# Two small first chunks, w_in in halves of columns, V by heads, and a new task list in an attention-then-MLP kernel

## The chip, the cores and the metric

The kernel runs on one core of a Trainium2 chip. The metric is device time in microseconds (us) for one launch. TensorE is called PE, VectorE DVE, ScalarE ACT, GpSimd POOL and SyncE SP, as in the profile.

## The reference

```python
def phi(x):                                   # 32 -> 64 features a token
    a = np.einsum('rd,bhsd->bhsr', S1, x)     # r = 8
    b = np.einsum('rd,bhsd->bhsr', S2, x)
    return np.einsum('bhsi,bhsj->bhsij', a, b).reshape(*x.shape[:-1], r * r)
q_p, k_p = phi(q), phi(k)                     # q, k, v: 4 x 4 x 1088 x 32, float32
kv  = np.einsum('bhsf,bhsd->bhfd', k_p, v)
z   = np.sum(k_p, axis=2)
num = np.einsum('bhsf,bhfd->bhsd', q_p, kv)
den = np.einsum('bhsf,bhf->bhs', q_p, z)[..., None] + 1e-06
x   = (num / den), heads side by side: 4352 tokens x 128
h   = x @ w_in                                # 128 x 2048
out = (h * sigmoid(h)) @ w_out                # 2048 x 128
```

Batch 0 has to be worked up into `x` before the MLP can start; the MLP of the first tokens then runs beside the attention of the later batches.

## The kernel before

Every step is a named task, and `ORDER` is a list of all tasks written out by hand. Each engine takes its instructions in the order in which its tasks stand there; the engines wait for each other by semaphores only where data or a buffer is needed. A name carries the batch (0 to 3) or chunk, and the piece.

Loads, all issued by SP: `LK`, `LQ`, `LV` (k, q, v of a batch), `LI` (w_in), `LO` (w_out). Each load's issue waits until the load eight places earlier has landed. `LV` loads V in four loads of 32 partitions each, all heads in one (`load_v`, line 207).

Attention of batch b, in pieces of 64-token groups (`PIECES`; batch 0 has three pieces, the first of 384 tokens):

- `KT` transposes k (DVE), `PK` projects it (PE, into the PSUM tile `pair`), `TK` transposes it back (DVE), `KP` forms the features (DVE for batch 0, POOL in nine parts for the others), `VB` casts V (ACT for batches 0 and 1), `KV` sums k features times v (PE), `KM`, `SE`, `KC` mask, select and copy that sum into the tile `KV`. `ZS`, `ZT`, `MW`, `WM` make the weights for the denominator.
- For each piece of q: `QT` transposes (DVE), `PQ` projects (PE, into `pair`), `TQ` transposes back (DVE, reads `pair`), `AW`, `RD`, `RC`, `AQ` form and apply the reciprocal of the denominator, `QP` forms the features, `TN` transposes them (all DVE), `NM` multiplies with `KV` (PE, into `pair`), and `XC` copies the result as bf16 into `xT` (ACT for batches 0 and 1, DVE for 2 and 3).

So `pair` is taken in turn by `PK`, `PQ` and `NM`, and freed by `TK`, `TQ` and `XC`.

MLP: the tokens are cut into chunks (`SIZES`). For a chunk, `H` multiplies with columns of w_in into one of two PSUM tiles `hp`, `A` applies silu on ACT (two, four or eight columns blocks at once, up to 1,024 elements a partition), `O` multiplies with w_out and accumulates, `F` writes out. From chunk 7 on (`H3`) `pair` is a third tile for `H`. `wi` casts w_in in four quarters on ACT, `wo` casts w_out on POOL. `H0.0` needs the first columns of w_in and `XC0.0`.

`f.0` to `f.106` are matmuls on zeros on PE, whose results nobody reads. They stand in the list up to the first chunk. All matmuls have one line in the profile, 181, as they go through one helper; products on DVE and POOL have line 192.

Of the kernel before, what the change touches and what calls it, by code (L numbers as in the profile page):

```python
# [40 lines left out]
SIZES = [384, 512, 512, 512, 512, 512, 512, 512, 256, 128]  # L41
NG = 8
PIECES = [[(0, 6), (6, 12), (12, 17)], [(0, 8), (8, 17)], [(0, 8), (8, 17)], [(0, 8), (8, 17)]]
KN = [[('D', 0, 5), ('D', 5, 9)], [('P', 0, 1), ('P', 1, 2), ('P', 2, 3), ('P', 3, 4), ('P', 4, 5), ('P', 5, 6), ('P', 6, 7), ('P', 7, 8), ('P', 8, 9)], [('P', 0, 1), ('P', 1, 2), ('P', 2, 3), ('P', 3, 4), ('P', 4, 5), ('P', 5, 6), ('P', 6, 7), ('P', 7, 8), ('P', 8, 9)], [('P', 0, 1), ('P', 1, 2), ('P', 2, 3), ('P', 3, 4), ('P', 4, 5), ('P', 5, 6), ('P', 6, 7), ('P', 7, 8), ('P', 8, 9)]]
XENG = ['AAA', 'AA', 'DD', 'DD']
KVENG = 'AADD'
VB_ENG = 'AAPP'
FILL = {'f.0': (1, 128), 'f.1': (1, 128), 'f.2': (1, 128), 'f.3': (1, 128), 'f.4': (1, 128), 'f.5': (1, 128), 'f.6': (1, 128), 'f.7': (1, 128), 'f.8': (1, 128), 'f.9': (1, 128), 'f.10': (1, 128), 'f.11': (1, 128), 'f.12': (1, 128), 'f.13': (1, 128), 'f.14': (1, 128), 'f.15': (1, 128), 'f.16': (1, 128), 'f.17': (1, 128), 'f.18': (1, 128), 'f.19': (1, 128), 'f.20': (1, 128), 'f.21': (1, 128), 'f.22': (1, 128), 'f.23': (1, 128), 'f.24': (1, 128), 'f.25': (1, 128), 'f.26': (1, 128), 'f.27': (1, 128), 'f.28': (1, 128), 'f.29': (1, 128), 'f.30': (1, 128), 'f.31': (1, 128), 'f.32': (1, 128), 'f.33': (1, 128), 'f.34': (1, 128), 'f.35': (1, 128), 'f.36': (1, 128), 'f.37': (1, 128), 'f.38': (1, 128), 'f.39': (1, 128), 'f.40': (1, 128), 'f.41': (1, 128), 'f.42': (1, 128), 'f.43': (1, 128), 'f.44': (1, 128), 'f.45': (1, 128), 'f.46': (1, 128), 'f.47': (1, 128), 'f.48': (1, 128), 'f.49': (1, 128), 'f.50': (1, 128), 'f.51': (1, 128), 'f.52': (1, 128), 'f.53': (1, 128), 'f.54': (1, 128), 'f.55': (1, 128), 'f.56': (1, 128), 'f.57': (1, 128), 'f.58': (1, 128), 'f.59': (1, 128), 'f.60': (1, 128), 'f.61': (1, 128), 'f.62': (1, 128), 'f.63': (1, 128), 'f.64': (1, 128), 'f.65': (1, 128), 'f.66': (1, 128), 'f.67': (1, 128), 'f.68': (1, 128), 'f.69': (1, 128), 'f.70': (1, 128), 'f.71': (1, 128), 'f.72': (1, 128), 'f.73': (1, 128), 'f.74': (1, 128), 'f.75': (1, 128), 'f.76': (1, 128), 'f.77': (1, 128), 'f.78': (1, 128), 'f.79': (1, 128), 'f.80': (1, 128), 'f.81': (1, 128), 'f.82': (1, 128), 'f.83': (1, 128), 'f.84': (1, 128), 'f.85': (1, 128), 'f.86': (1, 128), 'f.87': (1, 128), 'f.88': (1, 128), 'f.89': (1, 128), 'f.90': (1, 128), 'f.91': (1, 128), 'f.92': (1, 128), 'f.93': (1, 128), 'f.94': (1, 128), 'f.95': (1, 128), 'f.96': (1, 128), 'f.97': (1, 128), 'f.98': (1, 128), 'f.99': (1, 128), 'f.100': (1, 128), 'f.101': (1, 128), 'f.102': (1, 128), 'f.103': (1, 128), 'f.104': (1, 128), 'f.105': (1, 128), 'f.106': (1, 128)}
# [4 lines left out]
WIN = 1  # L53
ENDS = 2
LAST = [8, 6, 2]
DIRECT = [8, 9]
OPS = [5, 7, 9]
H3 = 7
ORDER = """
S2 LK0.0 LK0.1 begin KT0.0 KT0.1 LQ0.0 QT0.0 LV0.0 LV0.1 LV0.2 LV0.3 begin2 S1 f.0 f.1 f.2 f.3 f.4 f.5 f.6  # L60
f.7 f.8 f.9 SM SN table WQ0 WK L4 f.10 f.11 f.12 f.13 f.14 f.15 f.16 f.17 f.18 f.19 f.20 f.21 f.22 f.23 f.24
PK0.0 PK0.1 TK0.0 TK0.1 f.25 f.26 f.27 f.28 f.29 f.30 f.31 f.32 f.33 ZS0 ZT0 f.34 f.35 f.36 f.37 f.38 f.39
f.40 f.41 MW0 WM0 f.42 f.43 f.44 f.45 f.46 f.47 f.48 f.49 f.50 PQ0.0 KP0.0 KP0.5 TQ0.0 AW0.0 RD0.0 RC0.0
AQ0.0 QP0.0 TN0.0 VB0 f.51 f.52 f.53 f.54 f.55 f.56 f.57 f.58 KV0.0 KV0.5 KM0 f.59 f.60 f.61 f.62 f.63 f.64
f.65 f.66 f.67 SE0 KC0 f.68 f.69 f.70 f.71 f.72 f.73 f.74 f.75 f.76 f.77 f.78 f.79 f.80 f.81 f.82 f.83 f.84
f.85 f.86 f.87 f.88 f.89 f.90 NM0.0 LI.0 wi.0 wi.2 wi.3 XC0.0 wi.1 LQ0.1 LO.0 LO.1 wo.1 wo.0 wo.2 wo.3 WR
LK1 LV1.0 LV1.1 LV1.2 LV1.3 QT0.1 QT0.2 f.91 f.92 f.93 f.94 f.95 f.96 f.97 f.98 f.99 f.100 PQ0.2 TQ0.2 AW0.2
RD0.2 RC0.2 f.101 H0.0 H0.1 A0.0 f.102 PQ0.1 f.103 f.104 f.105 f.106 H0.2 O0.0 A0.1 TQ0.1 AW0.1 AQ0.2 RD0.1
QP0.2 RC0.1 TN0.2 AQ0.1 KT1 QP0.1 LQ1 LK2 LV2.0 LV2.1 LV2.2 LV2.3 LQ2 LK3 H0.3 A0.2 O0.1 H0.4 A0.3 A0.4 O0.2
H0.5 A0.5 NM0.2 O0.3 H0.6 XC0.2 H0.7 A0.6 A0.7 PK1 O0.4 O0.5 O0.6 TK1.1 TK1.0 TN0.1 KP1.0 KP1.1 KP1.2 KP1.3  # L70
KP1.4 KP1.5 KP1.6 KP1.7 KP1.8 ZS1 VB1 ZT1 NM0.1 O0.7 MW1 KV1.0 WM1 QT1.0 LV3.0 LV3.1 LV3.2 LV3.3 LQ3 XC0.1
H1.0 A1.0 H1.1 KV1.1 KV1.2 PQ1.0 KV1.3 KV1.4 H1.2 F0 QT1.1 O1.0 A1.1 KV1.5 H1.3 A1.2 A1.3 TQ1.0 AW1.0 RD1.0
KT2 RC1.0 KV1.6 O1.1 H1.4 O1.2 KV1.7 KV1.8 H1.5 PK2 A1.4 KM1 A1.5 H1.6 SE1 O1.3 O1.4 O1.5 H1.7 AQ1.0 QP1.0
TK2.0 TK2.1 TN1.0 A1.6 KC1 NM1.0 XC1.0 A1.7 O1.6 ZS2 PQ1.1 H2.0 ZT2 A2.0 O1.7 H2.1 KT3 TQ1.1 AW1.1 F1 MW2
PK3 WM2 RD1.1 RC1.1 TK3.1 AQ1.1 QP1.1 TK3.0 TN1.1 QT2.0 QT3.0 A2.1 H2.2 A2.2 KP2.0 KP2.1 KP2.2 KP2.3 KP2.4
KP2.5 VB2 KP2.6 KP2.7 VB3 KP2.8 KP3.0 KP3.1 KP3.2 KP3.3 KP3.4 KP3.5 KP3.6 KP3.7 KP3.8 H2.3 O2.0 A2.3 KV2.0
KV2.1 KV2.2 KV2.3 KV2.4 KV2.5 O2.1 H2.4 O2.2 A2.4 H2.5 O2.3 KV2.6 KV2.7 NM1.1 H2.6 A2.5 H2.7 KV2.8 O2.4
XC1.1 A2.6 ZS3 PQ2.0 ZT3 A2.7 KM2 H3.0 O2.5 O2.6 O2.7 SE2 H3.1 TQ2.0 AW2.0 QT2.1 RD2.0 RC2.0 F2 A3.0 A3.1
H3.2 KC2 PQ2.1 MW3 A3.2 KV3.0 H3.3 A3.3 KV3.1 O3.0 H3.4 KV3.2 O3.1 H3.5 O3.2 A3.4 A3.5 TQ2.1 AQ2.0 QP2.0
TN2.0 H3.6 A3.6 NM2.0 XC2.0 AW2.1 RD2.1 RC2.1 AQ2.1 QP2.1 TN2.1 KV3.3 H3.7 A3.7 O3.3 KV3.4 H4.0 O3.4 KV3.5  # L80
H4.1 O3.5 A4.0 KV3.6 H4.2 A4.1 O3.6 H4.3 O3.7 KV3.7 A4.2 H4.4 A4.3 NM2.1 KV3.8 H4.5 F3 WM3 XC2.1 O4.0 A4.4
A4.5 H4.6 PQ3.0 H4.7 O4.1 A4.6 H5.0 QT3.1 TQ3.0 PQ3.1 AW3.0 TQ3.1 KM3 RD3.0 AW3.1 RC3.0 A4.7 H5.1 A5.0 O4.2
H5.2 O4.3 SE3 KC3 AQ3.0 QP3.0 TN3.0 RD3.1 A5.1 H5.3 A5.2 O4.4 H5.4 O4.5 O4.6 A5.3 H5.5 A5.4 O4.7 H5.6 NM3.0
O5.0 A5.5 H5.7 XC3.0 RC3.1 A5.6 A5.7 O5.1 H6.0 O5.2 O5.3 H6.1 A6.0 O5.4 H6.2 A6.1 A6.2 AQ3.1 QP3.1 TN3.1 F4
NM3.1 O6.0 XC3.1 H6.3 O5.5 A6.3 H6.4 A6.4 O5.6 H7.0 A7.0 H6.5 O6.1 H6.6 O6.2 O6.3 O5.7 A6.5 H6.7 H7.3 A6.6
F5 A6.7 H7.1 A7.1 A7.3 O6.4 O6.5 H7.2 O6.6 O7.0 H7.4 O6.7 H7.6 A7.2 H7.5 O7.1 A7.4 A7.6 H7.7 O7.2 O7.3 O7.4
A7.5 F6 A7.7 H8.0 A8.0 H8.1 O7.5 H8.2 O7.6 A8.1 A8.2 H8.3 A8.3 O7.7 H9.0 O8.0 O8.1 H9.1 O8.2 O8.3 H9.2 A9.0
F7 A9.1 A9.2 O9.0 O9.1 O9.2 F8 F9
# [4 lines left out]
def kernel(  # L93
# [77 lines left out]

    def load(name, make):
        def issue():
            landed[name] = make()
            if name in HOLDS:
                tc.add_manual_dep(landed[name].ins, landed[HOLDS[name]].ins.name, mybir.DependencyInfo(
                    mybir.DependencyClass.Sync, mybir.DependencyReason.DATA), reason="order of loads")
        o.add(name, issue)

    def mm(dst, w, x, start=True, stop=True, pos=None, **kw):  # L180
        nc.tensor.matmul(dst, w, x, start=start, stop=stop, tile_position=pos, **kw)  # L181
# [25 lines left out]
    def load_v(b, c):  # L207
        n = min(NC, NY - c * NC)
        return nc.sync.dma_start(
            view(Vx[b % 2][32 * c: 32 * (c + 1), :], 0, (NC * D, H), (1, n * D)),  # L210
            AP(tensor=v.tensor, offset=v[b, 0, c * NC].offset,
               ap=[[NY * D, 32], [S * D, H], [1, n * D]]))

    quarter = DFF // 4
    YQ = 2 * PIECES[0][0][1]
    load("LK0.0", lambda: load_rows(k, Kx, 0, 0, 2 * NC, by[K_ENG]))
    load("LK0.1", lambda: load_rows(k, Kx, 0, 2 * NC, NY))
    load("LQ0.0", lambda: load_rows(q, Qx, 0, 0, YQ))
    load("LQ0.1", lambda: load_rows(q, Qx, 0, YQ, NY))
    for b in range(B):  # L220
        for c in range(4):
            load(f"LV{b}.{c}", lambda b=b, c=c: load_v(b, c))
# [3 lines left out]
    for i in range(WIN):  # L226
        r0, r1 = i * P // WIN, (i + 1) * P // WIN
        load(f"LI.{i}", lambda r0=r0, r1=r1: nc.sync.dma_start(w_in_f[r0:r1, :], moe_w_in[r0:r1, :]))
# [32 lines left out]
    def begin2():  # L261
        nc.gpsimd.tensor_copy(out=view(SEL[:, :], 0, (P, 2), (64, 2), (1, 64)),
                              in_=view(ident[:, :], 0, (1, 2), (0, 2), (2, 64)))
        nc.gpsimd.memset(view(Vx[1][96:P, :], (NY - 3 * NC) * D, (NC * D, H),
                              (1, (4 * NC - NY) * D)), 0.0)
        nc.gpsimd.memset(view(AW[1][:, :], 8, (9, 2 * NN)), 1e-6)
        for b in range(1, B):
            nc.gpsimd.memset(view(WQ[b][:, :], 16, (32, 2), (1, 16)), 0.0)
            nc.gpsimd.memset(view(Kx[b][:, :], NY * D, (1, (4 * NC - NY) * D)), 0.0)
    o.add("begin2", begin2)  # L270
# [75 lines left out]
    def batch(b, kn, pieces, xeng, kveng):  # L346
# [72 lines left out]
        for p, (n0, n1) in enumerate(pieces):  # L419
# [3 lines left out]

            o.add(f"QT{b}.{p}", lambda n0=n0, n1=n1: nc.vector.transpose(  # L424
                out=qt[:, n0 * 64: n1 * 64], in_=Qx[b][:, n0 * 64: n1 * 64]))

            def project_q(n0=n0, m=m):
                for c in range(2):
                    for r in range(2):
                        mm(pair[64 * c: 64 * (c + 1), r * CH: r * CH + m * 32],  # L430
# [156 lines left out]
```

## Time and profile before

| | |
|---|---|
| time of 3 runs, us | 94.51, 94.75, 96.81; median 94.75 |
| profiled execution | 95.22 us, of which the span from first to last instruction is 93.4 |
| busy in the span | PE 87.5 us (94%), ACT 76.3 (82%), DVE 59.3 (63%), POOL 26.4 (28%) |
| matmuls on zeros | 107, 10.1 us busy |
| first matmul of the MLP (`H0.0`) | 15.52 us |
| first silu | 16.05 us |
| first silu of a full chunk (`A1.0`) | 25.31 us |
| last matmul's start group, last copy of the output | 89.04, 90.13 us |

Times in the text are us from the start of the span, unless they are said to be of a launch. Busy times of PE are modelled for pipelined matmuls and overlap a little; the distance from one start to the next says more. A line of the timeline gives start, length, engine, line of the kernel, operation, output and inputs, shapes, how many instructions were merged, and in square brackets how long the engine was idle before and for whom it waited.

### The profile page before, as it was taken

Reading aid. Unit: us, or ns where it says so; the run is one execution under the profiler, and the core shown is the slowest. Engines: PE = TensorE matmul, PEld = TensorE weight load, DVE = VectorE, ACT = ScalarE, POOL = GpSimd, SP = SyncE. Lnnn points to the kernel's source line nnn. Section 1 sums busy time; section 2 is a strip of 40 time slices with the busy share of each in tenths; the row PEclk is TensorE's granted clock in tenths of the full one; section 3 lists DMA queues with packets and bytes.
Section 4 is the critical chain, followed back from the end, with each engine's and each line's share of the span. In section 5 each row is a group of like instructions: output and inputs, shape, how many; then the busy total and the mean of one; then the engine's idle time right before and its main releaser. Section 6 shows DMA issues by size and latency. Waiting matters only on the chain.

```text
span 93.4 us, 2184 instructions
## 1 busy us (share of the span) xinstructions
PE 87.5 (94%) x813; PEld 46.7 (50%) x823; DVE 59.3 (63%) x114; ACT 76.3 (82%) x102; POOL 26.4 (28%) x91
## 2 busy tenths in 40 slices
PE   5999989999999999999999999999999999999950
PEld 4948776544543443544444443344344444456940
DVE  2369796999499969983986978489597030300330
ACT  4800687999599868899699999999898999999930
POOL 6700008300993299999900000000000000000000
PEclk9999999999999999999999999999999999999999
DMA  0999999999968730600024003300001404133151
GB/s 19 334 256 343 374 408 318 245 291 238 309 202 222 229 77 14 112 0 7 0 39 73 0 0 63 56 0 0 0 0 29 70 14 85 34 56 60 31 115 50
DMA packets 21898, 11.15 MB, mean 119 GB/s; under 512 B 17152, under 2 KB 20608, under 8 KB 21760
## 3 DMA queue, kind: packets, MB, share of 16 engines
q1 hardware_dynamic: 21704, 10.95, 44.7%
q8 instruction: 6, 0.10, 0.4%
q10 hardware_dynamic: 184, 0.07, 0.3%
q14 instruction: 4, 0.03, 0.1%
HBM read 8.79 MB, written 2.23 MB: 118 GB/s over the span
## 4 chain that ended last, share of the span: by engine, by line
PE 83%; DVE 9%; issue 2%; POOL 2%; DVEq 0%; POOLq 0%
PE hp L181 28%; PE op L181 27%; PE pair L181 14%; PE small L181 14%; DVE QP L192 2%; DVE TQ L435 2%; DVE QU L455 2%; DVE AW L192 1%; DVE TK L368 1%; DVE DN L442 1%; DVE DN L445 1%; DVE AQ L192 0%; POOL hmask L245 0%; POOL Vx L251 0%; DVE OT L540 0%
## 5 line engine op out<-in xcount | busy, mean ns | idle before, releaser
L519 ACT ACTIVATE G<-hp 128x1024 bf16<-128x1024 f32 (+1 forms) x66 | 60.9, 989 | 4.6 <-PE hp L181 2.9
L181 PE MATMUL hp<-xT,w_in_bf 128*128 128x512 bf16 (+3 forms) x137 | 36.2, 355 | 0.2
L181 PE MATMUL op<-G,w_out_bf 128*128 128x512 bf16 (+1 forms) x93 | 25.8, 370 | 0.2
L181 PEld LDWEIGHTS <-w_in_bf 128*128 128x128 bf16 x160 | 13.7, 98 | 13.3 <-issue 2.8
L192 POOL TENSOR_TENSOR KP<-TK 128x256 bf16<-128x256 f32 x27 | 17.0, 631 | 9.2 <-DVE TK L368 9.2
L181 PEld LDWEIGHTS <-w_out_bf 128*128 128x128 bf16 x128 | 11.6, 98 | 12.5 <-issue 1.1
L181 PE MATMUL op<-zeros 128*128 128x128 bf16 x107 | 10.1, 255 | 1.0 <-DVE zeros L240 1.0
L192 DVE TENSOR_TENSOR QP<-AQ,TQ 128x1024 bf16<-128x1024 f32 (+3 forms) x9 | 10.8, 1195 | 0.2
L181 PEld LDWEIGHTS <-zeros 128*128 128x128 bf16 x107 | 7.9, 116 | 3.0 <-issue 1.7
L181 PE MATMUL small<-G,w_out_bf 128*128 128x512 bf16 x31 | 8.8, 379 | 0.1
L435 DVE STREAM_TRANSPOSE TQ<-pair 128x512 f32<-128x512 f32 (+3 forms) x9 | 6.1, 675 | 3.7 <-PE pair L181 2.8
L546 DVE STREAM_TRANSPOSE OT<-small 128x512 f32<-128x512 f32 x2 | 1.4, 716 | 9.3 <-PE small L181 9.3
L355 DVE STREAM_TRANSPOSE KT<-Kx 128x1152 f32<-128x1152 f32 (+1 forms) x5 | 5.6, 1135 | 2.2 <-DMA Kx<-in_k_dram 2.1
L546 DVE STREAM_TRANSPOSE OT<-op 128x512 f32<-128x512 f32 (+1 forms) x6 | 4.0, 667 | 4.1 <-PE op L181 4.1
L181 PEld LDWEIGHTS <-KP 128*128 128x128 bf16 x72 | 4.3, 98 | 4.0 <-issue 0.4
L455 DVE STREAM_TRANSPOSE QU<-QP 128x512 f32<-128x512 f32 (+3 forms) x9 | 6.0, 665 | 0.2
L424 DVE STREAM_TRANSPOSE QT<-Qx 128x512 f32<-128x512 f32 (+3 forms) x9 | 5.7, 653 | 0.3 <-DMA Qx<-in_q_dram 0.3
L181 PE MATMUL pair<-QT,WQ 64*64 64x256 f32 (+3 forms) x72 | 5.7, 389 | 0.1
L181 PE MATMUL small<-Vb,KP 128*128 128x64 bf16 x72 | 5.3, 193 | 0.1
L519 ACT ACTIVATE G<-pair 128x1024 bf16<-128x1024 f32 x5 | 5.2, 1037 | 0.0
L189 POOL CAST w_out_bf<-w_out_f 128x512 bf16<-128x512 f32 x4 | 2.3, 612 | 9.9 <-DMA w_out_f<-in_moe_w_out_dram 9.9
L187 DVE CAST xT<-pair 128x512 bf16<-128x512 f32 (+4 forms) x6 | 3.4, 615 | 2.2 <-PE pair L181 2.2
(68 smaller groups left out, 73.0 us busy)
## 6 DMA issues: line engine op xcount, KB each, us to landing
Vx<-in_v_dram SPq DMA_DIRECT2D x12, 144.0 KB, 9.1
Kx<-in_k_dram SPq DMA_DIRECT2D x3, 544.0 KB, 12.3
Qx<-in_q_dram SPq DMA_DIRECT2D x3, 544.0 KB, 8.8
w_in_f<-in_moe_w_in_dram SPq DMA_DIRECT2D x1, 1024.0 KB
w_out_f<-in_moe_w_out_dram SPq DMA_DIRECT2D x2, 512.0 KB, 9.2
out_dram<-OT SPq DMA_DIRECT2D x16, 64.0 KB, 1.9
Vx<-in_v_dram SPq DMA_DIRECT2D x4, 112.0 KB, 7.2
Qx<-in_q_dram SPq DMA_DIRECT2D x1, 352.0 KB, 7.8
```

The lines of the kernel that those rows point to most:

```text
L181: nc.tensor.matmul(dst, w, x, start=start, stop=stop, tile_position=pos, **kw)
L187: nc.vector.tensor_copy(out=out_, in_=in_)
L189: nc.gpsimd.tensor_copy(out=out_, in_=in_)
L192: (nc.vector if eng == "D" else nc.gpsimd).tensor_tensor(out=out_, in0=a, in1=c, op=ALU.mult)
L355: o.add(f"KT{b}{at}", lambda c0=c0, c1=c1: nc.vector.transpose(out=view(kt[:, :], c0 * 32, (32, c1 - c0), (P, NC), (1, 32)), in_=Kx[b][:, ...
L368: o.add(f"TK{b}.{r}", lambda r=r: nc.vector.transpose(out=view(tk[:, :], 16 * r, (32, NC), (NC * 32, 2), (1, 16)), in_=view(pair[:, :], r ...
L424: o.add(f"QT{b}.{p}", lambda n0=n0, n1=n1: nc.vector.transpose(out=qt[:, n0 * 64: n1 * 64], in_=Qx[b][:, n0 * 64: n1 * 64]))
L435: o.add(f"TQ{b}.{p}", lambda at=at, m=m: nc.vector.transpose(out=tq[:, at * 32: (at + 2 * m) * 32], in_=view(pair[:, :], 0, (CH, 2), (1, m ...
L442: o.add(f"RD{b}.{p}", lambda at=at, rn=rn: nc.vector.tensor_reduce(out=dn[:, at: at + rn], in_=view(aw[:, :], at * 9, (9, rn), (1, 9)), ax ...
L455: o.add(f"TN{b}.{p}", lambda at=at, rn=rn: nc.vector.transpose(out=qu[:, at * 64: (at + rn) * 64].bitcast(FP32), in_=qp[:, at * 64: (at + ...
L519: nc.scalar.activation(out=view(gb[:, :], 0, (stride, per), (1, ntok)), in_=view(hb[:, :], 0, (stride, per), (1, ntok)), func=ACT.Silu)
L546: nc.vector.transpose(out=t[:, :ntok], in_=ob[:, :ntok])
```

## The change

- `SIZES`: the first chunk of 384 tokens becomes one of 128 (two groups of eight column blocks) and one of 256 (four groups of four). All later chunks cover the tokens they did, with numbers one higher. `PIECES` of batch 0: the first piece of 384 tokens is cut into 128 and 256.
- `WIN = 2`: w_in is loaded in two halves of its columns instead of one load.
- `V_BY = 'head'`: V of a batch comes in five loads: one for each head into 96 partitions (1,152 bytes each), and the last rows of all heads into 32 partitions as before.
- `ORDER` is new throughout, with 73 matmuls on zeros instead of 107. Among the moves: `wi.1` and `wi.0` stand between `VB0` and `KM0`, `wi.2` ahead of `KC0`; `PQ0.1` stands ahead of `KV0`; `XC0.1` stands ahead of `A0.1`; `VB1` directly ahead of the first silu of a full chunk (`A2.0`); `KT2` ahead of `TQ1.0`, where it stood behind `RD1.0`; `PQ3.0` to `XC3.1` come later against the chunks.
- Code for cutting pieces further (`QCUT`, `XCUT`, a 17th group in `sp`) and for choosing engines (`AENG`, `QENG`) is added. With the values given, no piece has more than 9 groups, each is cut into one part, and the engines are those of before.

```diff
-SIZES = [384, 512, 512, 512, 512, 512, 512, 512, 256, 128]
+SIZES = [128, 256, 512, 512, 512, 512, 512, 512, 512, 256, 128]
-PIECES = [[(0, 6), (6, 12), (12, 17)], [(0, 8), (8, 17)], ...
+PIECES = [[(0, 2), (2, 6), (6, 12), (12, 17)], [(0, 8), (8, 17)], ...
-WIN = 1
+WIN = 2
-DIRECT = [8, 9]
-OPS = [5, 7, 9]
-H3 = 7
+DIRECT = [9, 10]
+OPS = [6, 8, 10]
+H3 = 8
+V_BY = 'head'
+Y_Q = 12
+RING = 2
...
 def load_v(b, c):
+    if V_BY == "head" and c < H:
+        return nc.sync.dma_start(
+            Vx[b % 2][:3 * 32, c * NC * D: (c + 1) * NC * D],
+            AP(tensor=v.tensor, offset=v[b, c, 0].offset,
+               ap=[[NC * D, 3], [NY * D, 32], [1, NC * D]]))
+    c = min(c, 3)
     n = min(NC, NY - c * NC)
...
-        r0, r1 = i * P // WIN, (i + 1) * P // WIN
-        load(f"LI.{i}", ... w_in_f[r0:r1, :], moe_w_in[r0:r1, :]
+        c0, c1 = i * DFF // WIN, (i + 1) * DFF // WIN
+        load(f"LI.{i}", ... w_in_f[:, c0:c1], moe_w_in[:, c0:c1]
```

The new list from the q side of batch 0 to the first full chunk, without the matmuls on zeros:

```
PQ0.0 TQ0.0 AW0.0 PQ0.1 RD0.0 RC0.0 TQ0.1 AQ0.0 AW0.1 QP0.0.0 RD0.1 RC0.1 TN0.0.0 AQ0.1 QT0.3 VB0 KV0.0 wi.1 wi.0
KV0.5 KM0 SE0 wi.2 KC0 NM0.0 wi.3 XC0.0.0 LK1 LV1.0 ... QP0.1.0 PQ0.3 QT0.2 TQ0.3 TN0.1.0 H0.0 PQ0.2 H0.1 A0.0
AW0.3 RD0.3 TQ0.2 RC0.3 AQ0.3 AW0.2 QP0.3.0 RD0.2 TN0.3.0 KT1 ... NM0.1 XC0.1.0 O0.0 H1.0 A0.1 A1.0 H1.1 NM0.3 O0.1
H1.2 RC0.2 F0 AQ0.2 QP0.2.0 XC0.3.0 A1.1 PK1 TK1.1 TK1.0 TN0.2.0 A1.2 H1.3 O1.0 O1.1 O1.2 A1.3 ZS1 NM0.2 ZT1 O1.3
MW1 KP1.0 ... KP1.8 QT1.0 WM1 F1 KT2 XC0.2.0 VB1 H2.0 A2.0 LV3.0 ... H2.1 PQ1.0 KV1.0 KV1.1 KV1.2 KV1.3 KV1.4 H2.2
O2.0 A2.1 KV1.5 H2.3 A2.2 A2.3 TQ1.0 PK2 H2.4
```

## Prediction

> **What bounds the kernel now.** I read the busy time by stretches first, then the start of PE, ACT and DVE in order of time, then the SP queue with the landings.
>
> ```profile
> 15.00:25.00 10.00, 9.59 (x113) 4.94 (x113) 7.67 (x19) 8.49 (x13) 3.72 (x12) 1.00 1.06 266
> 25.00:46.00 21.00, 20.75 (x213) 9.39 (x217) 18.05 (x35) 17.99 (x22) 17.73 (x49) 1.00 0.41 108
> 46.00:65.00 19.00, 18.89 (x133) 8.18 (x134) 14.91 (x29) 18.58 (x20) 0.80 (x4) 1.00 0.17 28
> 65.00:90.00 25.00, 24.84 (x181) 13.67 (x181) 8.31 (x15) 23.66 (x27) 0.00 (x0) 1.00 0.24 42
> ```
>
> The columns are length, then busy PE, PEld, DVE, ACT, POOL, clock, DMA share, GB/s. From 25 us on PE is full (98 to 99%), and 83% of the chain that ended last is PE. So from there the end moves only as much as PE's useful work starts earlier or stalls. Before 25 us PE is filled with matmuls on zeros. This is PE there (start, length, operands, count):
>
> ```profile
> 8.11 0.98 PE L181 MATMUL op<-zeros 128*128 128x128 bf16 x8
> 9.02 0.29 PE L181 MATMUL small<-ZT,L 128*64 128x16 f32 x4
> 9.25 0.68 PE L181 MATMUL op<-zeros 128*128 128x128 bf16 x9
> ...
> 14.06 0.36 PE L181 MATMUL pair<-QU,KV 64*64 64x192 bf16 x8 [0.21 <-DVE QU L455]
> ...
> 15.52 0.81 PE L181 MATMUL hp<-xT,w_in_bf 128*128 128x384 bf16 x4
> ```
>
> A fill costs 0.114 us up to about 9 us (8.18 to 9.09 in the chain for 8) and 0.068 after it. NM0.0 at 14.06 waits for TN0.0; H0.0 at 15.52 waits for ACT:
>
> ```profile
> 12.61 0.38 ACT L185 ACTIVATE KV<-small 128x256 bf16<-128x256 f32 x1 [0.36 <-PE small L181]
> 12.89 1.66 ACT L185 ACTIVATE w_in_bf<-w_in_f 128x512 bf16<-128x512 f32 x3
> 14.48 0.49 ACT L185 ACTIVATE xT<-pair 128x384 bf16<-128x384 f32 x1
> 14.86 0.62 ACT L185 ACTIVATE w_in_bf<-w_in_f 128x512 bf16<-128x512 f32 x1
> ...
> 25.31 1.02 ACT L519 ACTIVATE G<-hp 128x1024 bf16<-128x1024 f32 x1 [0.81 <-PE small L181]
> ```
>
> The last cast of w_in ends at 15.48 and H0.0 follows. The first silu of a full chunk, A1.0, starts at 25.31 (its H1.0 at 24.61). In the new kernel the same chunk is number 2, so H2.0 and A2.0 are to be held against these two.
>
> **The change, step by step.** Durations by width: DVE transposes take 0.43, 0.52, 0.58, 0.70, 0.78 us at 288, 320, 384, 512, 576 columns, 1 ns a column, so I estimate 0.33 for 128 and 0.45 for 256. QP takes 0.82, 0.96, 1.22 at 640, 768, 1024, so 0.42 for 256 and 0.69 for 512. PQ takes 0.50, 0.56, 0.63 at 160, 192, 256, so 0.34 for 64 and 0.44 for 128.
>
> *To NM0.0.* One more fill stands before ZS0 (+0.11), four fewer before MW0 (-0.46): MW0 at 8.75, not 9.09; WM0 9.1 to 9.5; PQ0.0 at 9.6, not 9.99. TQ0.0 is then held by KP0 on DVE, which ends at 10.22: 10.2, not 10.60. From TQ0.0 to TN0.0 DVE now has 8 instructions for two tokens' pieces interleaved with 3 of the second piece, instead of 7 on 384 tokens in 3.4 us; their sum is 2.7, so TN0.0 ends at 12.9. The other input is KV: PQ0.1 (10.6 to 11.05) stands ahead of KV0 (0.65) on PE, KM0 starts at 11.8 (now 11.73), and one cast, wi.2, stands ahead of KC0 on ACT, which ends at 13.1 (now 12.99). NM0.0 at 13.15, held by KC0.
>
> *The w_in halves.* wi.1 and wi.0 move in front of KM0, from 12.89 to about 10.55 to 11.7. They cost nothing if the first half has landed by 10.5. The packets of w_in run from 6.4 to 10.7 us in the trace, so the first half ends near 8.6, and 0.4 to 0.9 us from last packet to semaphore (K's first half 3.53 to 3.88, Q's 4.84 to 5.76) still fits. The second half is needed at 12.2. Without this cover KM0 and all behind it on ACT would wait. wi.3 (0.62) ends at 13.6 ahead of XC0.0 (estimate 0.28): 13.9. PQ0.3 then takes `pair`, 13.95 to 14.45, and H0.0 starts at 14.45: 1.07 us earlier than 15.52.
>
> *H0.0 to H2.0.* Here time goes back. After A0.0 (14.95 to 15.95) ACT stands at XC0.1, which waits for NM0.1, which waits for TQ0.2 to free `pair`: TQ0.3 14.5, TN0.1, AW0.3, RD0.3, TQ0.2 at 15.75 to 16.1, end 16.3 to 16.7, NM0.1, XC0.1 until 17.15 to 17.5. The spread is w_out's casts on POOL: an AW beside them took 0.69 us, and 0.26 without. A0.1 is queued behind XC0.1, and H1.1 waits for A0.1. Then A0.1, A1.0, XC0.3, A1.1, A1.2, A1.3 run on ACT for about 4.9, ZS1 and NM0.2 come on PE at 22.3 to 23.3, XC0.2 until 23.5 to 23.85, H2.0 at 23.6 to 24.0, and VB1 (1.16) stands between XC0.2 and A2.0: 24.5 to 24.9. PE's work from H0.0 to H2.0 is 7.8 us in 9.3; before it was 7.9 in 9.1. The gain is now 0.65 to 1.0. The extra weight loads of the 128-token chunk are free: 16 such matmuls take 0.89 us at the end of the kernel, as long as their columns need.
>
> *The second batch's K.* On DVE the transpose KT2 now stands ahead of TQ1.0; before it stood behind TQ1.0, AW1.0 and RD1.0 (line by line below), when its data had been there for a while.
>
> ```profile
> 26.72 0.67 DVE L435 STREAM_TRANSPOSE TQ<-pair 128x512 f32<-128x512 f32 x1
> 27.43 0.29 DVE L192 TENSOR_TENSOR AW<-TQ 128x128 f32<-128x128 f32 x1
> 27.76 0.30 DVE L442 TENSOR_REDUCE DN<-AW 128x16 f32<-128x144 f32 x1
> 27.98 1.37 DVE L355 STREAM_TRANSPOSE KT<-Kx 128x1152 f32<-128x1152 f32 x1
> ```
> ```profile
> Qx<-in_q_dram SPq DMA_DIRECT2D x1, 544.0 KB, 10.6
> ...
> Kx<-in_k_dram SPq DMA_DIRECT2D x1, 544.0 KB, 12.7
> ```
>
> These are the loads issued between 13 and 15 us, with the time to landing; K of batch 2 is issued at 14.05 (SP queue), so it lands at 26.75. In the new kernel DVE comes to KT2 at about 24.2. If it lands at L, KT2 ends at L+1.38, TQ1.0 at L+2.0, and PK2, which needs `pair` free, runs from L+2.05 to L+2.7; H2.4 and all of PE stand behind it. Before, PE had done the same work (four H, one O, six KV, PQ1.0, PK2) at 30.52 less two H, two O and three KV, 1.93: 28.6. So the gain at this point is 25.9 - L, and never above 0.65 to 1.0.
>
> How early L comes hangs on V by heads, for the DMA engines are full until then (9 in all of slices 1 to 10 of the page's DMA row, 2.3 to 25.7 us). V's packets of 1,152 B take 71 ns on average, 51 at the lower quartile. Only the four head loads, 384 packets a batch, get a new shape; the fifth keeps 32 partitions. The upper bound of the saving is 384 x 20 ns / 16 engines = 0.48 us a batch, and two batches of V lie ahead of K2: L = 25.8. The lower bound is nothing: L = 26.75. K2's issue, which waits for the landing eight loads back, moves from w_out's first half (landed 14.08) to its second (15.6); the engines still have two loads before it, so that is hidden. I take 25.8, as 1,024 B packets to all partitions take 46 ns.
>
> The Trainium skill, "SBUF — State Buffer", section "Door 1: The DMA port swizzle", speaks against hoping for more: partitions 0 to 63 reach no more DMA ports than 0 to 31, and only 64 up reach the other half. By it 64 of a head's 96 partitions stay on the old ports, a third of the load leaves them, 0.57 us a batch, L = 25.6 and a gain of 0.3.
>
> *After PK2.* Both orders have the same PE work left, 58.3 us summed from 0.4315 us a pair of 512-wide matmuls and the attention rows; before takes 59.6. I find one new wait, PQ2.0 behind XC1.1 on ACT, 0.3 us, and no other where DVE's sum exceeds PE's between producer and consumer (NM3.0 has only 0.2 us of slack). I set the two lists equal, between +0.7 and -0.9.
>
> *Sum.* 93.4 - (25.9 - 25.8) = 93.3 us of span. The profiled execution took 95.22, 1.82 outside the span, and stands 0.47 above the median 94.75: 95.1 there, 94.6 as a median.
>
> **Rivals.** (1) *K2 lands by 25.0*: the lag between fast and slow DMA engines (V of batch 2 starts on some at 20.2, while K2 ends near 26 on others) shrinks as V spreads. For: that lag; against: even at 51 ns a packet only 0.96 us are to be had. Gain 0.65 to 1.0: 93.9. (2) *K2 lands as today*, slower than before: V's shape gains nothing, DVE stands at KT2 until 26.75, PK2 ends at 29.45, 0.85 late: 95.6. It decides from L = 25.9 on. For: two thirds of a head keep old partitions; against: full-width packets are cheaper in every row. (3) *TensorE's clock falls back.* The cold half of the start shows the price: PK0 took 1.48 us against 0.72 for PK1. With 34 fewer fills, PE waits about PQ0.2, NM0.1 and H1.1. From H0.0's end at 14.9 to H1.1's end at 18.5 I count 2.8 us of PE work; at half rate it takes 5.6, 2.0 more than the 3.6: 96.6. Against: it is busy for 78% of that stretch, and 15 to 25 was 96% busy without a drop. The Trainium skill, "TensorE: Matmul & The Clock Gate", Part 1, has half rate only after an idle window of about 3.4 us; by that rule no drop. (4) *The new list also ends stalls after PK2*: 1.3 us at most, with rival 1's gain 92.7.
>
> **How the numbers follow.** Forecast 0.35; rivals 0.23, 0.18, 0.12, 0.12. Low end 93.0 (rival 1 with the +0.7 gives 93.2, rival 4 lies below), high end 96.4 (rival 2 with -0.8, the lower half of rival 3): about 0.1 is left out on each side. A difference of 2% is about what a measurement of this kernel can tell from none; below 92.85 lies most of rival 4 and a little of rival 1, 0.15; above 96.65 half of rival 3 and the tail of rival 2, with stalls I did not find, 0.15.
>
> **What would show it.** Right: H0.0 near 14.45, ACT idle for about 1 us ahead of XC0.1, A2.0 at 24.5 to 24.9, DVE waiting for Kx at KT2, PK2 at 27.85. Wrong: KM0 waiting for w_in; no DMA wait at KT2; matmuls of 128 columns at 0.11 us after 15 us; PE stalls of over 1 us in all after 29.

## The result: slower by a tenth

The changed kernel takes 103.88 us (median of four runs, 103.54 to 105.03); the kernel before, on the same chip, 94.70. The ratio is 1.100, with a 95% interval of 1.089 to 1.110. The forecast was 94.6 with a range of 93.0 to 96.4: wrong in sign and size. Medians here are over all runs of a kernel; ratios leave out runs that were disturbed, so the two need not match to the last digit.

The profiled execution took 103.86 us with a span of 101.9, 8.5 more than before. The first view is again busy time by stretches (length, busy PE, PEld, DVE, ACT, POOL, clock, DMA share, GB/s), of the changed kernel:

```profile
15.00:25.00 10.00, 9.50 (x123) 6.91 (x128) 7.29 (x19) 6.83 (x13) 2.34 (x4) 0.74 0.70 237
25.00:46.00 21.00, 18.52 (x214) 8.62 (x199) 15.30 (x30) 15.57 (x21) 13.24 (x37) 0.95 0.43 125
46.00:65.00 19.00, 19.00 (x155) 8.30 (x154) 14.80 (x25) 16.93 (x20) 7.75 (x19) 0.96 0.30 68
65.00:90.00 25.00, 25.00 (x144) 10.73 (x143) 12.33 (x24) 23.76 (x26) 0.00 (x0) 1.00 0.19 32
90.00:101.90 11.90, 8.53 (x95) 6.50 (x93) 2.15 (x4) 8.05 (x10) 0.00 (x0) 1.00 0.31 61
```

From 65 us on nothing is wrong: PE is full at full clock, the work only comes later. The damage is done in two places. From 15 to 25 us the clock column reads 0.74 and the DMA share has fallen from 1.06 to 0.70 although loads are waiting; from 25 to 46 PE is idle for 2.5 us. PE and ACT in order of time show both places (the last line is ACT of the kernel before):

```profile
10.49 0.45 PE L179 MATMUL pair<-QT,WQ 64*64 64x128 f32 x8 [0.29 <-DVE TQ L457]
14.37 1.12 PE L179 MATMUL small<-Vb,KP 128*128 128x64 bf16 x18 [3.43 <-ACT Vb L191]
...
18.74 1.03 PE L179 MATMUL hp<-xT,w_in_bf 128*128 128x128 bf16 x8
...
28.66 1.04 PE L179 MATMUL hp<-xT,w_in_bf 128*128 128x512 bf16 x4
...
32.34 0.72 PE L179 MATMUL pair<-KT,WK 64*32 64x288 f32 x16 [0.30 <-DVE TQ L457]
...
42.99 0.72 PE L179 MATMUL pair<-KT,WK 64*32 64x288 f32 x16 [2.19 <-DVE TQ L457]
```
```profile
13.16 1.16 ACT L191 ACTIVATE Vb<-Vx 128x1152 bf16<-128x1152 f32 x1 [4.06 <-DMA Vx<-in_v_dram]
```
```profile
9.74 1.16 ACT L185 ACTIVATE Vb<-Vx 128x1152 bf16<-128x1152 f32 x1
```

First place: the cast of batch 0's V stands until 13.16, where it began at 9.7 before, because V has not landed. `KV0.0` (14.37) waits 3.43 us for it, and H0.0 comes at 18.74 instead of 15.52. Second place: PK3 at 42.99 is held for 2.19 us by TQ1.1 on DVE, and DVE in order of time says why TQ1.1 is late:

```profile
30.31 1.38 DVE L367 STREAM_TRANSPOSE KT<-Kx 128x1152 f32<-128x1152 f32 x1 [0.43 <-DMA Kx<-in_k_dram]
...
40.30 1.38 DVE L367 STREAM_TRANSPOSE KT<-Kx 128x1152 f32<-128x1152 f32 x1 [3.40 <-DMA Kx<-in_k_dram]
```

KT3, ahead of TQ1.1 on DVE, stands 3.40 us for K of batch 3. The SP queue of the changed kernel shows that this load was issued at 30.73; before (the last line) it was at 21.20.

```profile
10.16 2.91 SPq L209 DMA_DIRECT2D Kx<-in_k_dram  x1
13.12 5.26 SPq L216 DMA_DIRECT2D Vx<-in_v_dram  x4
...
21.52 6.72 SPq L216 DMA_DIRECT2D Vx<-in_v_dram  x4
...
30.73 0.43 SPq L209 DMA_DIRECT2D Kx<-in_k_dram  x1
```
```profile
21.20 0.35 SPq L203 DMA_DIRECT2D Kx<-in_k_dram  x1
```

The four head loads of batches 1 and 2 hold SP for 5.3 and 6.7 us. It is not the wait for the load eight places back that fills this time: of these eight issues one alone, at 23.80, starts as that load lands. The issue itself is long, up to 2.79 us with a median of 0.75 over all head loads; what holds it, no view shows. All of it points at V by heads, and one column says what is the matter with it. This is the stretch from 5.2 to 6.2 us, when V of batch 0 is on the way, in the kernel before and then in the changed one; the last two columns are DMA share and GB/s:

```profile
5.20:6.20 1.00, 1.00 (x17) 0.36 (x16) 0.67 (x2) 0.00 (x0) 0.00 (x0) 1.00 1.06 235
```
```profile
5.20:6.20 1.00, 1.00 (x16) 0.28 (x16) 0.71 (x3) 0.00 (x0) 0.00 (x0) 1.00 0.20 73
```

A share of 0.20 of 16 DMA engines is 3.2 engines. A head's source is walked as `[[NC*D, 3], [NY*D, 32], [1, NC*D]]`: its outermost step has 3 places. So the theory was: only three engines share a head load, and 384 packets at 51 to 54 ns each (median and mean of batch 0 in the trace) take 384 x 0.052 / 3 = 6.7 us a batch. These 384 packets of batch 0 do lie between 4.56 and 11.93 us, 7.4 us in all; the 384 packets of that size before lay between 4.20 and 6.72.

### The profile page after: what moved, and what is told of

It is laid out like the page before. It is cut to its first block, busy times and chain, and to the rows that moved or that the text cites. A ratio compares the mean times of both kernels' runs of the same rounds, so it can differ in the third digit from the quotient of the medians.

```text
span 101.9 us, 2249 instructions
## 1 busy us (share of the span) xinstructions
PE 90.1 (88%) x837; PEld 48.1 (47%) x837; DVE 60.2 (59%) x123; ACT 76.6 (75%) x101; POOL 27.1 (27%) x91
## 4 chain that ended last, share of the span: by engine, by line
PE 54%; DMA 27%; SPq 13%; DVE 2%; issue 1%
PE hp L179 21%; PE op L179 16%; DMA Vx<-in_v_dram 15%; PE small L179 10%; DMA Qx<-in_q_dram 8%; PE pair L179 7%; SPq L216 7%; SPq L209 4%; DMA out_dram<-OT 3%; SPq L222 2%; DVE TQ L457 1%; DVE QT L439 1%; SPq L202 0%; DVE OT L577 0%
## 5 line engine op out<-in xcount | busy, mean ns | idle before, releaser
L179 PE MATMUL hp<-xT,w_in_bf 128*128 128x512 bf16 (+2 forms) x158 | 38.2, 346 | 0.3 <-ACT G L556 0.3
L179 PE MATMUL op<-G,w_out_bf 128*128 128x512 bf16 (+2 forms) x112 | 26.8, 351 | 0.0
L198 DVE TENSOR_TENSOR QP<-AQ,TQ 128x1024 bf16<-128x1024 f32 (+5 forms) x10 | 10.6, 1063 | 0.2
L457 DVE STREAM_TRANSPOSE TQ<-pair 128x512 f32<-128x512 f32 (+5 forms) x10 | 6.2, 619 | 4.8 <-PE pair L179 4.8
L439 DVE STREAM_TRANSPOSE QT<-Qx 128x512 f32<-128x512 f32 (+5 forms) x10 | 6.0, 603 | 5.1 <-DMA Qx<-in_q_dram 5.1
L583 DVE STREAM_TRANSPOSE OT<-op 128x512 f32<-128x512 f32 (+2 forms) x7 | 4.2, 602 | 6.9 <-PE op L179 6.9
L179 PE MATMUL pair<-QT,WQ 64*64 64x256 f32 (+5 forms) x80 | 6.4, 393 | 0.5 <-DVE TQ L457 0.3
L482 DVE STREAM_TRANSPOSE QU<-QP 128x512 f32<-128x512 f32 (+5 forms) x10 | 6.1, 606 | 0.1
L179 PE MATMUL pair<-KT,WK 64*32 64x288 f32 x64 | 3.7, 482 | 2.5 <-DVE TQ L457 2.5
L191 ACT ACTIVATE Vb<-Vx 128x1152 bf16<-128x1152 f32 x2 | 2.3, 1159 | 4.1 <-DMA Vx<-in_v_dram 4.1
```

The source lines that it names most:

```text
L191: nc.scalar.activation(out=out_, in_=in_, func=ACT.Copy)
L198: (nc.vector if eng == "D" else nc.gpsimd).tensor_tensor(out=out_, in0=a, in1=c, op=ALU.mult)
L457: nc.vector.transpose(out=tq[:, at * 32: (at + 2 * m0) * 32], in_=view(pair[:, :], 0, (CH, 2), (1, m0 * 32)))
L482: o.add(f"TN{b}.{p}.{s}", lambda x=at + s0, z=at + s1: nc.vector.transpose(out=qu[:, x * 64: z * 64].bitcast(FP32), in_=qp[:, x * 64: z * ...
L583: nc.vector.transpose(out=t[:, :ntok], in_=ob[:, :ntok])
```

## The experiments

### Is it V by heads?

Three edits tell V's load from the list and the halves. The rivals were the new list (DVE standing at KT2, the waits before H2.0) and the clock.

`e1_v_chunks`, the changed kernel with V loaded as before:

```diff
-V_BY = 'head'
+V_BY = 'chunk'
```

> The changed kernel with V in the four loads of before (32 partitions, all heads), the rest of the change kept. Three-engine theory (a head load runs on 3 of the 16 DMA engines because the outermost step of its source is 3): no stretch with 3 packets in flight, VB0 at 9.4 to 9.8, H0.0 near 14.5, a launch of 93.9 to 95.6 us, as the step-by-step sum gave without a gain from V. Rival, the new list itself is bad: over 99 us. Rival, TensorE's clock falls because 34 matmuls on zeros are gone: clock under 0.97 and 96.5 or more.

Measured: 96.26 us in the median of four runs, ratio to the kernel before 1.013 (0.995 to 1.030). That is at or a little above the upper end of the theory, and far from the first rival; the clock was 1.0.

`e2_before_v_heads`, the kernel before with V by heads alone:

```diff
+        if V_BY == "head" and c < H:
+            return nc.sync.dma_start(Vx[b % 2][:3 * 32, ...],
+                AP(..., ap=[[NC * D, 3], [NY * D, 32], [1, NC * D]]))
```

> The kernel before with only V loaded by heads (five loads a batch). Three-engine theory: each batch of V takes 384 packets x 51 ns / 3 = 6.5 us instead of 2.2, so VB0 waits until 12 to 13.5 us (9.7 before), later batches are late too, 99 to 105 us. Rival, the new list is bad and V harmless: 94 to 95.5 us.

Measured: 103.17 us, ratio 1.092 (1.072 to 1.112). Its V cast starts at 13.56 after 4.03 us of waiting for V, and its DMA share from 5.2 to 6.2 us is 0.19.

`e3_v_32_outer`, the changed kernel with the two outer steps of the source exchanged, the same packets into the same 96 partitions. The rows of V then lie in another order than those of K, so this kernel does not compute the reference; it and the later ones with 32 outermost serve for the time alone:

```diff
-                   ap=[[NC * D, 3], [NY * D, 32], [1, NC * D]]))
+                   ap=[[NY * D, 32], [NC * D, 3], [1, NC * D]]))
```

> The changed kernel; the source of a head load is walked with 32 as the outermost step and 3 inside, so the same bytes go to the same 96 partitions in packets of the same size, with the rows in another partition order (the sums over k and v pair other rows, so the output's numbers differ). Three-engine theory: 16 packets in flight during the head loads, VB0 by 9.8, 93 to 95.5 us. Rival, 96 partitions as such are slow (two thirds of them on the ports of the first 64): as the changed kernel, 102 to 105 us.

Measured: 95.89 us, ratio 1.011 (1.002 to 1.019). V alone brings the whole loss into the old list, and taking it away, or only exchanging two steps of its walk, takes the loss out of the new list. So the loss is not the 96 partitions, nor five loads instead of four, nor the list, up to the 1% that is left (95.89 us is a little above the 95.5 that the theory allowed).

### Is it the number of engines?

`e6_v_6_outer` changes the one number in dispute:

```diff
-                   ap=[[NC * D, 3], [NY * D, 32], [1, NC * D]]))
+                   ap=[[17 * NC * D, 6], [NC * D, 16], [1, NC * D]]))
```

> The changed kernel, with the outermost step of a head's source walk of 6 instead of 3 (6 x 16 rows, the same 384 packets of 1,152 B a batch into the same 96 partitions; the rows that land are other rows of V, so the result is not V's). Theory (the outermost step of the source sets how many DMA engines share the load): 6 packets in flight while head loads run, 384 x 51 ns / 6 = 3.3 us a batch, V of batch 0 cast from about 9.5 to 10.5 instead of 13.16, time between 95.5 and 98.5. Rival (96 partitions as such, or any walk that does not run 32 rows first, is slow): 3 in flight, the cast near 13, time 102 to 104.

Measured: 98.44 us in its one run, the upper end of what the theory gave and 3.6 us below the rival. V's cast starts at 10.08. (Part of the 2.7 us of span over `e3` is the granted clock, 0.67 from 15 to 25 us, after PE had waited 2.11 us for ACT at 14.42; the engine count below does not hang on that.) The stretch from 5.2 to 6.2 us of this run:

```profile
5.20:6.20 1.00, 1.00 (x18) 0.40 (x16) 0.90 (x3) 0.00 (x0) 0.00 (x0) 1.00 0.39 138
```

0.39 of 16 is 6.2 engines: the share doubled with the step, and the rate nearly so, 138 GB/s for 73. The trace has a second count. The semaphore that tells of a load's landing was updated 4 times for each head load of the change, once soon after the issue and 3 times later; 7 times in `e6` (1 and 6); and 16 times in `e3`, as for every load of K, Q, w_in and w_out. That settles it: with 96 partitions on the other side, the outermost step of the source sets how many engines work. The Trainium skill says so in "DMA: Bandwidth & Descriptors", section "Why a DMA increments its semaphore by 16 and not by 1": of both sides' patterns the slowest dimension longer than one is taken, and the largest number up to 16 that divides both sizes is the number of engines. With 96 partitions on one side and 3 or 6 on the other that gives 3 and 6, and the traces agree (0.20 and 0.39 of 16).

### How does a late V become 9 us?

Two experiments each took one link out of the chain. `e4_more_fills` keeps PE's clock up while it waits for V of batch 0, with 50 matmuls on zeros between `PQ0.1` and `KV0.0`:

```diff
-... AQ0.1 QT0.3 VB0 KV0.0 ...
+... AQ0.1 QT0.3 VB0 g.0 g.1 ... g.49 KV0.0 ...
```

> The changed kernel with 50 more matmuls on zeros between PQ0.1 and KV0.0, about the 3.4 us in which PE is idle for V. Theory that the loss is the wait for V and the clock only follows it: the granted clock stays 1.0 from 12.7 to 20.4 us, H0.0 comes about 0.8 us earlier (the work between 14.4 and 18.7 at full rate), 1 to 2 us less than the changed kernel, 102 to 103. Rival, the lost clock is the main cost: under 99 us.

Measured: 103.76 us, ratio 1.086 (1.062 to 1.109). The clock row shows no drop before 43 us any more, and the time is much the same: neither the 1 to 2 us of the theory nor the rival came. The interval leaves room for a gain of up to 3 or 4%, but not for the clock being the main part. PE of its profiled execution (104.38 us) shows where the gain goes:

```profile
17.62 0.62 PE L180 MATMUL hp<-xT,w_in_bf 128*128 128x128 bf16 x8
...
27.02 1.04 PE L180 MATMUL hp<-xT,w_in_bf 128*128 128x512 bf16 x3
29.40 0.66 PE L180 MATMUL pair<-QT,WQ 64*64 64x256 f32 x8 [1.34 <-DVE WQ L199]
...
32.17 0.72 PE L180 MATMUL pair<-KT,WK 64*32 64x288 f32 x16 [0.36 <-DVE TQ L458]
...
43.40 1.22 PE L180 MATMUL pair<-KT,WK 64*32 64x288 f32 x16 [2.76 <-DVE TQ L458]
```

H0.0 is 1.12 us earlier than in the change and H2.0 (27.02) 1.64. Then PE waits for DVE, which had stood 3.08 us for Q of batch 1; PK2 is only 0.17 earlier, and PK3 is not earlier at all, as DVE stands at KT3 until 40.71.

`e8_v0_chunks` loads V of batch 0 as before and the other three by heads:

```diff
-        if V_BY == "head" and c < H:
+        if V_BY == "head" and b and c < H:
...
-        for c in range(5 if V_BY == "head" else 4):
+        for c in range(5 if V_BY == "head" and b else 4):
```

> The changed kernel, with V of batch 0 alone loaded in four chunk loads as before, batches 1 to 3 by heads. It tells apart the first wait (V of batch 0) and the later loads behind V of batches 1 to 3. Theory A (the first wait and the clock drop behind it make most of the loss, about 6 of 9 us): H0.0 near 14.5 to 15, time 96 to 98.5. Theory B (each batch of V holds up the K and Q behind it and the loss is shared out or even mostly in the later batches): H0.0 near 14.5 to 15 all the same, but K of batches 2 and 3 wait as in the changed kernel (5.9 us in 3 stops), time 99 to 103.

Measured: 99.35 us, ratio 1.041 (1.034 to 1.049): just inside theory B. (H0.0 comes at 15.47, later than either theory had it.) About two fifths of the loss are left with V of batch 0 on time. Its chain of waits and its PE, each in order of time, show what the later batches cost:

```profile
27.07 10.25 DMA Kx<-in_k_dram
...
37.41 0.10 DVE KT L367
```
```profile
40.10 0.72 PE L179 MATMUL pair<-KT,WK 64*32 64x288 f32 x16 [2.50 <-DVE TQ L457]
```

The transpose KT3 starts at 37.41 in this run, as soon as K of batch 3 is there, and PE stands 2.50 us at PK3.

The runs of the new list can now be laid beside each other at PK2 (the first matmul group on batch 2's K) and the end of the span:

| | PK2 starts | end of span | from PK2 to the end | idle at PK3 |
|---|---|---|---|---|
| V on 16 engines (`e3`) | 28.11 | 93.7 | 65.6 | none |
| V on 6 engines (`e6`) | 30.79 | 96.4 | 65.6 | none |
| V of batches 1 to 3 on 3 engines (`e8`) | 29.14 | 97.2 | 68.1 | 2.50 |
| the change, all on 3 engines | 32.34 | 101.9 | 69.6 | 2.19 |

From PK2 on the list takes 65.6 us unless it stands at PK3. The 8.2 us between the change and `e3` are 4.2 up to PK2, 2.2 of standing at PK3, and 1.8 more behind it, where the granted clock was 0.50 from 44.5 to 46.5 us, which it was not in `e8`.

The first two are not separate causes. `e4` shows that the clock up to there is not what counts: with PE 1.64 us ahead at H2.0, the later loads hold it just the same. That PE's first wait would be swallowed in the same way is argued from this; no run takes it away without a faster load. PK3 comes when K of batch 3 does (KT3 at 40.30 in the change, 40.71 in `e4`, 37.41 in `e8`). So the loss runs through the loads. V of batch 0 carries somewhat over half of it, 4.7 us by the spans of the change and `e8`: without its slow load K of batch 3 is there 2.9 us sooner, and the 1.8 behind PK3 are gone. The other 3.5 us are 2.50 at PK3, for K of batch 3 behind the head loads of batches 1 and 2, and 1.0 up to PK2, which no run takes apart.

### What is the rest of the change worth?

`e9_before_v_32_outer` puts V by heads on 16 engines into the kernel before:

```diff
+                AP(..., ap=[[NY * D, 32], [NC * D, 3], [1, NC * D]]))
```

> The kernel before, with V by heads into 96 partitions as the only edit, and the source walked with the 32 as outermost step (so that all 16 DMA engines share a head; the rows come permuted). It measures what the new shape is worth in itself, which the prediction bounded between nothing and 0.48 us a batch. Theory (96 partitions cost no more than 32, the change's loss lay in the walk alone): K of batch 2 lands 0 to 1 us earlier than 26.75, time 0.99 to 1.00 of the kernel before. Rival (the shape costs something in itself, five loads and their issue instead of four): 1.01 or more.

Measured: ratio 0.999 (0.996 to 1.003). The page's table of loads gives, for the three whole batches of K, the median time from issue to landing as its last number, here of this run:

```profile
Kx<-in_k_dram SPq DMA_DIRECT2D x3, 544.0 KB, 7.9
```

Before it was 12.3. For batch 2 the issue came 2.75 us later (16.80 instead of 14.05) and the load took 4.7 us less, so K landed about 2 us sooner. No one was waiting for it: the time stays.

`e11_v_32_outer_again` is `e3` in more rounds, the whole change but for the three engines:

> The changed kernel with the head loads walked 32 outermost and the halves kept, in more rounds: all of the change but the three engines. The prediction's 94.6 against 94.75 would be 0.998 of the kernel before; three rounds gave 1.0107, between 1.0023 and 1.0191. Theory (the prediction's walk misses about 0.5 us: H2.0 at 24.80 where 23.6 to 24.0 was worked out, and the lists are not equal after): 1.003 to 1.010. Rival (equal, as predicted): 0.996 to 1.002.

Measured: 1.006 (1.002 to 1.010), within the first theory. Three runs take it apart. `e5_win2_only` is the kernel before with w_in in two halves:

```diff
-WIN = 1
+WIN = 2
...
-        r0, r1 = i * P // WIN, (i + 1) * P // WIN
+        c0, c1 = i * DFF // WIN, (i + 1) * DFF // WIN
```

> The kernel before, with w_in loaded in two halves of columns instead of one piece and nothing else. The casts of w_in stand at 12.89 us there, after all of w_in has landed, so the halves have nothing to serve. Theory (halves as such are free): 0.995 to 1.003 of the kernel before. Rival (one load more in SP's queue and the eight-deep window makes the loads behind it, K of batch 1 first, come later, and the first chunks wait): 1.005 to 1.015.

Measured: 1.0045 (1.0008 to 1.0081), a small loss, between theory and rival. `e7_list_only` is the new list and chunks with V and w_in loaded as before (`V_BY = 'chunk'`, `WIN = 1`, `LV*.4` and `LI.1` dropped from the list):

> The changed kernel without V by heads (four chunk loads) and without the halves of w_in (one load): the two chunks of 128 and 256 tokens and the new list alone. Prediction's view (the lists are equal after the second batch's K, the halves serve the casts that stand ahead of KM0): the casts wait for all of w_in, KM0 past 12.5 instead of 11.8, NM0.0 near 13.9, time 1.00 to 1.01. Rival (the new list in itself is slower, for DVE and PE stand at KT2 and the like; the halves do not matter): 1.01 to 1.02, the same as with halves (1.012). Second rival (the halves hurt, as the loads behind them come later): below 1.00.

Measured: 1.0025 (0.997 to 1.008). `e10_v_32_one_w_in` is `e3` with `WIN = 1`:

> The changed kernel with the head loads walked 32 outermost (16 engines, rows permuted) and w_in in one piece: chunks, list and V's shape without the halves. Theory (the casts ahead of KM0 need the early first half, and lose 0.5 to 1 us without it): KM0 past 12.5, time 0.3 to 1 us above the run with halves below. Rival (the halves cost what they bring): the same as with halves, within 0.3 us, or below.

Measured: 1.011 (1.004 to 1.019). Its interval overlaps with `e11`'s and with `e7`'s, so whether the halves help or hurt the time in the new list stays open; the ratios lie within 1% of each other. The wait that both texts expected is there: with w_in in one load ACT stands for it 1.39 us in `e7` and 2.18 in `e10`, and KM0 starts at 13.06 and 14.00, in profiled executions of 96.83 and 97.75 us.

Last, `e12_k1_ahead`, `e3` with one load moved, tries a cause for the remaining half per cent: K of batch 1 lands late (DVE starts KT1 at 19.40 in `e3`, at 19.88 after 1.02 us of waiting in `e11`), and H2.0 with it.

```diff
-... LQ0.1 LO.0 LO.1 ... XC0.0.0 LK1 LV1.0 ...
+... LQ0.1 LO.0 LK1 LO.1 ... XC0.0.0 LV1.0 ...
```

> The changed kernel with the head loads walked 32 outermost (16 engines, rows permuted), and K of batch 1 issued between the two halves of w_out instead of behind them. Theory (what is left of the loss, 1.0058 of the kernel before, is K of batch 1 landing at 19.4 to 19.9 us, with DVE standing for it): it lands up to 1 us earlier, DVE does not stand at that transpose, H2.0 at 24.3 to 24.8, time 0.998 to 1.004. Rival (w_out's second half then lands as much later, O0.1 waits for its casts, and the stand only moves): 1.005 to 1.012.

Measured: 1.009 (1.005 to 1.012), no better. The transpose no longer stands (it starts at 18.17), but PE in order of time shows that the rival came true:

```profile
19.46 0.40 PE L179 MATMUL op<-G,w_out_bf 128*128 128x128 bf16 x4 [0.46 <-POOL w_out_bf L195]
20.02 0.40 PE L179 MATMUL op<-G,w_out_bf 128*128 128x128 bf16 x4 [0.16 <-POOL w_out_bf L195]
...
24.66 1.04 PE L179 MATMUL hp<-xT,w_in_bf 128*128 128x512 bf16 x3
```

O0.1 now stands twice for the casts of w_out's second half, which landed later. While the DMA engines are full, a load that is moved up pushes another back. No version here is faster than the kernel before.

## Why the prediction was wrong

**The failed step: V by heads, in the part on the second batch's K.** The prediction bounded the new shape between a saving of 0.48 us a batch and nothing, by "384 x 20 ns / 16 engines". Both ends took for granted that 16 engines share a load. The packets' own price was not the trouble: 57 ns on average over the four batches of the change, between the 51 and 71 that the prediction reckoned with. The divisor was 3. Worked out as the runs show it, 384 packets take 6.7 us a batch; for batch 0 they took 7.4, where they had taken 2.5 before. In the kernel before only the loads of `S`, of 4 KB, have an outermost step under 16 (it is 8), so the trace could not give the price, but the bound then had no right to leave out a loss. The change wrote a new access pattern, and only its packets were costed, not who carries them. The page of the Trainium skill named above states the rule; the prediction drew on another page, on the ports of partitions, by which the change looked 0.2 us better still.

**To NM0.0, and H0.0 to H2.0.** With the engines restored (`e3`), the walk held up to H0.0 and a little beyond. This is PE of that run:

```profile
13.32 0.26 PE L179 MATMUL pair<-QU,KV 64*64 64x64 bf16 x8 [0.19 <-ACT KV L191]
...
14.44 0.62 PE L179 MATMUL hp<-xT,w_in_bf 128*128 128x128 bf16 x8
...
19.30 0.33 PE L179 MATMUL pair<-QU,KV 64*64 64x160 bf16 x8 [0.40 <-DVE QU L482]
...
20.93 0.72 PE L179 MATMUL pair<-KT,WK 64*32 64x288 f32 x16 [0.30 <-DVE DN L470]
...
24.80 1.04 PE L179 MATMUL hp<-xT,w_in_bf 128*128 128x512 bf16 x3
...
28.11 0.72 PE L179 MATMUL pair<-KT,WK 64*32 64x288 f32 x16
```

NM0.0 was worked out at 13.15, H0.0 at 14.45, the end of XC0.1 at 17.15 to 17.5 (it is 17.33). H2.0 was worked out at 23.6 to 24.0 and is at 24.80. Two stands that the walk did not have make 0.70 us of that: NM0.3 waits 0.40 for TN0.3, which is late because QP0.3 took 1.23 us on DVE for the 0.82 it was priced at (w_out's casts ran on POOL beside it), and PK1 waits 0.30 for DVE, which reached KT1 at 19.40, when K of batch 1 landed. That K is issued at 8.91 instead of 6.46, behind one V load and one w_in load more; the prediction counted SP's queue for K of batch 2 only. `e12` shows that the two stands can't be mended one at a time: with K of batch 1 early, others of 0.62 us take their place. In the changed kernel itself all of this is covered by V's delay.

**The w_in halves.** The first half was put at 8.6 us plus latency, from packets that ran from 6.4 to 10.7 when w_in was one load. In `e3` the cast stands for it until 10.92, 0.63 us. KM0 came at 11.97 for 11.8, so the miss cost little. Alone the halves cost 0.4%, not nothing.

**A misreading ahead of it all.** The prediction read H0.0 at 15.52 in the kernel before as waiting for the last cast of w_in, which ends at 15.48. H0.0 needs only the first quarter; what it stood behind was PQ0.2 on PE, which waited for XC0.0. Two times that lie 0.04 us apart are no proof of a wait.

**The second batch's K.** The wait named, DVE at KT2 with TQ1.0 and PK2 behind it, is there in the changed kernel, for 0.43 us at 30.31, and is a trifle. With 16 engines K lands in time in `e3` (no wait at KT2), as rival 1 had it, and nearly so in `e11`, the same kernel (0.32 us, at 26.31). But H2.0's delay had used up that gain: PK2 at 28.11 in `e3`, worked out at 27.85. That the two are so close is luck: H2.0 was 0.8 us or more too late, and K 0.8 too early, for the walk.

**After PK2** the two lists were set equal. From the predicted PK2 to the predicted end are 65.45 us; `e3` and `e6` take 65.6. This step held to 0.15 us in these two runs.

**The rivals.** None had the cause. Rival 3, the clock, did come, but as a consequence and at another place than argued: in PE's 3.43 us of idling before `KV0.0`, and again after the stand at PK3. The marks that the prediction set against itself were good: half-rate matmuls after 15 us (H0.0's eight take 0.83 us from start to start of the next group, 0.10 each) and more than 1 us of stalls after 29 both appear.

## What to carry to other kernels

Cost a new DMA pattern by three numbers, not one: how many packets, how long one takes, and how many engines share them; here a first step of 3 on the DRAM side left three, though the other side had 96 partitions. Look at the DMA share of the profile in the stretch of one load: 0.19 or 0.20 while loads wait is about three engines of sixteen. And when an edit can only be bounded because no row shows it, let the bound reach below nothing, however small the edit looks in the diff.

## What was not expected of the hardware

- With destination and packets unchanged, the number of engines followed the walk of the source: exchanging 3 and 32 brought the kernel from 103.9 to 95.9 us.
- With 16 engines, V's packets of batch 0 took 59 ns on average into 96 partitions (`e3`) and 75 into 32 (the kernel before), and K of batch 2 landed about 2 us sooner (`e9`), more than the 0.96 us that the prediction gave as the most for two batches. It bought nothing there.
- A slow load is paid by the loads behind it: in `e8` V of batch 0 was on time, and PE still lost 2.50 us at 40 us, for K of batch 3 behind the head loads of batches 1 and 2.
- The clock does not follow the length of one gap. In the traces all its changes within a run lie whole steps of 3.41 us apart: in the change it fell to 0.50 at 13.37, 2.4 us into the gap that began at 10.94, rose at 20.20, fell at 44.09 and rose at 47.50. So it matters how a gap lies in the steps. PE was busy for 0.69 and 1.23 us in the steps that ended with these two drops (9.96 to 13.37 and 40.68 to 44.09). The 2.50 us of `e8` were split over two steps with 1.97 and 2.20 us busy, and nothing fell. A step of 1.98, with a gap of only 1.20, did end in a drop there (at 14.99), so what decides near 2 us stays open. The Trainium skill, "TensorE: Matmul & The Clock Gate", Part 1, has half rate after an idle window of about 3.4 us. The length agrees with the steps of 3.41 us; that the window must be idle does not, as PE was busy for part of each of these.
